# Reordering the first four feed-forward units and their transposes in a one-core attention and feed-forward kernel

## The chip, the cores and the metric

The kernel runs on one core of one Trainium2 chip. The metric is the device time of one execution in microseconds (us); the medians below are over several executions. The traces give a "span", from the first to the last instruction of the program; it is about 2 us shorter than the device time of the same execution.

Engine names: PE is TensorE, ACT ScalarE, DVE VectorE, POOL GpSimd, SP SyncE (here it only issues DMAs).

## The reference

```python
def reference(A_x, A_k_cache, A_v_cache, A_wq, A_wo, B_x, B_w_gate, B_w_up, B_w_down):
    # x: (1, 2048, 448); 16 query heads, 8 key/value heads of 256; F = 1792; all bf16
    xn = layernorm(x)
    s  = attention(xn, last 512 keys of k_cache and v_cache, wq, wo)   # [...] softmax, no mask
    g  = silu((gelu(xn @ w_gate) * (xn @ w_up)) @ w_down)
    return x + s * g
```

## The kernel before

Tokens come in 16 tiles of 128, and in 4 chunks of 512. A feed-forward *unit* is one block of 128 of the 1792 features for one chunk: 14 blocks times 4 chunks are 56 units. A unit holds two PSUM banks, one for the gate and one for the up product. Each product contracts 448 rows: three blocks of 128 (`NK = 3`) and a rest of 64. All matmuls take 64 rows, and the upper and lower half of the array work side by side on the two products. So a unit is two *passes*: the first with 8 matmuls (the rest and three blocks, two halves each), the second with 6, with the halves exchanged. For this, the rest of 64 columns of `xn` has to stand in both halves of the transposed tile `xnT`. The kernel before gets that by normalising those 64 columns twice, into a tile 512 wide:

```python
        def ln_norm(t):
            s = t % NXN
            for lo, hi, src in ((0, D, 0), (D, DP, K3)):       # 448 columns, then 64 again
                K.op("dve", lambda e, ...: e.tensor_scalar(xn[:, s, lo:hi], ...))

        def ln_tp_pe(t, b, eng):                               # tiles 0..3: transposed by PE
            for k in range(NK + 1):
                ins = e.transpose(tp[:, k * P:(k + 1) * P], xn[:, s, k * P:(k + 1) * P], ident[:, :])
            # [...] one copy PSUM -> xnT, on ACT
```

Tiles 4 to 15 are transposed by DMA (`ln_tp_dma`). At the start nothing is there yet, so three units begin at once and work through the first chunk tile by tile, in quarters of 128 columns (condensed):

```python
        warm(20, 3)                    # 20 matmuls on zeros
        ln_first(0); ln_first(1); ln_second(0); ln_second(1)
        ln_tp_pe(0, 6, "act")
        ln_stats(2); ln_std_act(2)     # a square root on ACT ahead of tile 1's copy
        ln_tp_pe(1, 7, "act")
        ln_first(3)
        HEAD, PH = (0, 1, 2), (0, 2, 4)          # units, and the first of their two banks
        gu_group(HEAD, PH, 0)                    # quarter 0 (token tile 0)
        gu_group(HEAD, PH, 1)                    # quarter 1
        # [...] DVE work
        ln_tp_pe(2, 6, "act"); ln_tp_pe(3, 7, "act")
        act(..., ACT.Gelu_apprx_tanh, ...)       # loads the Gelu table
        gu_group(HEAD, PH, 2); gu_group(HEAD, PH, 3)
        # [...]
        cur, nxt = (6, 0), (2, 4)
        for n in range(3, NU - 1, 2):            # pairs (3,4), (5,6), ...: unit 4 reuses unit 0's banks
            gu_group((n, n + 1), cur)
            gu_evac(n, cur[0])                   # Gelu on ACT, product on DVE
            ln_b()                               # normalise and DMA-transpose a coming tile
            gu_evac(n + 1, cur[1])
            ln_a()
            if n == 3:
                load_x("sp", 12, 4)
```

Unit 55 is left over and is woven into the first query heads. At the very end the last token tile's output projection runs as two halves of 224 columns, so that finishing the first half runs under the second. The program ends with `drain`: SP waits for the last DMA of each of its 16 slots, a slot being one semaphore; DMAs take the slots in turn.

The softmax here doesn't subtract the row's maximum and nothing guards it: scores larger than these inputs give would overflow.

## Time and profile before

| | |
|---|---|
| device time, median of the first 3 executions | 562.93 us (562.39 to 563.58) |
| span of the profiled execution | 560.8 us |
| PE busy | 555.0 us, 99% of the span |
| DVE / ACT / POOL busy | 279.5 / 211.5 / 32.7 us |
| chain of work that ended last | PE 98% |

These are lines of the page of the kernel before. The first two have one digit for each fortieth of the span, a tenth of full for each step: the busy share of PE, and of the DMA engines. The third is a DMA queue with its kind, packets, MB and share of the DMA engines' time. The fourth is the chain of work that ended last.

```profile
PE   8999999999999999999999999999999999999997
DMA  9910999300033034012331320144044012421331
q8 instruction: 33, 0.54, 0.4%
PE 98%; DVE 1%; DMA 0%; ACT 0%; issue 0%; DVEq 0%
```

PE is the bound everywhere, so only time in which PE starves can be won, and the only slices under 9 are the first and the last. The DMA engines are full in the first two slices (28 us). The queue called "instruction" brings PE's own program, in 33 packets of 16 KB.

This is the timeline of PE alone, before the change. The columns are start, duration, engine, line, operation, what was written and read, shape, how many were merged, and in brackets the idle time before it and what ended it.

```profile
5.71 0.40 PE L402 MATMUL bank<-ident,xn 128*128 128x128 bf16 x4 [0.18 <-DVE rstd L382]
6.79 0.23 PE L322 MATMUL bank<-xnT,wgur 64*128 64x128 bf16 x2
...
8.16 0.23 PE L322 MATMUL bank<-xnT,wgur 64*128 64x128 bf16 x2
...
9.44 0.62 PE L402 MATMUL bank<-ident,xn 128*128 128x128 bf16 x8
10.61 0.23 PE L322 MATMUL bank<-xnT,wgur 64*128 64x128 bf16 x2 [0.56 <-ACT xnT L316]
...
12.96 0.40 PE L322 MATMUL bank<-xnT,wgur 64*128 64x512 bf16 x2
13.17 0.83 PE L322 MATMUL bank<-xnT,wgu 64*128 64x512 bf16 x6
14.29 0.39 PE L322 MATMUL bank<-xnT,wgur 64*128 64x512 bf16 x2 [0.29 <-DVE actT L459]
14.52 0.81 PE L322 MATMUL bank<-xnT,wgu 64*128 64x512 bf16 x5
15.50 1.67 PE L322 MATMUL bank<-xnT,wgu 64*128 64x512 bf16 x13 [0.18 <-issue]
16.81 0.57 PE L322 MATMUL bank<-xnT,wgur 64*128 64x512 bf16 x2
...
19.84 0.57 PE L322 MATMUL bank<-xnT,wgur 64*128 64x512 bf16 x2
...
35.23 0.93 PE L322 MATMUL bank<-wd,actT 128*128 128x448 bf16 x4
```

Each group of units starts with the two matmuls on `wgur`, the rest of 64 rows, so these lines are markers: 6.79 is quarter 0, 8.16 quarter 1, 10.61 quarter 2, 12.96 the pair of units 3 and 4, 16.81 the pair 5 and 6, and from there a pair takes 3.02 us. The last line is the first work on the down weights. After the first transposes, three waits stand in the brackets: for the copies of the transposes (10.61), for the product that frees unit 0's bank (14.29), and one, at 15.50, in the middle of a unit, after the fifth of six matmuls, for nothing that the profile shows ("issue").

The end of the timeline of the kernel before, DVE's last two operations:

```profile
557.87 0.39 DVE L631 SCALAR_TENSOR_TENSOR tmp<-bank,g_58 128x224 f32<-128x224 f32 x1 [2.25 <-PE bank L322]
558.30 0.39 DVE L634 TENSOR_TENSOR ofin<-tmp,xr 128x224 bf16<-128x224 f32 x1
```

### The profile page before, as it was taken

To read this page: it belongs to the slowest core of one execution; us is meant where nothing else is said; L and a number is where in the kernel's file an instruction comes from. 1 tells how busy PE (TensorE), PEld (TensorE's weight loads), DVE (VectorE), ACT (ScalarE), POOL (GpSimd) and SP (SyncE) were. 2 spreads that over 40 slices of the span, in tenths; PEclk is the share of its full clock that TensorE was granted. 3 is DMA by queue.
4 is the path that set the end of the run, shared out by engine and by line. 5 is a ranking of instruction groups with operands and counts; after the bars stand their busy time and mean duration, and the time that the engine had idled before them with its cause. 6 is when DMAs were issued, how large, how long until landed. Compare 5 with 4: busy or idle time off the path is not lost.

```text
span 560.8 us, 9965 instructions
## 1 busy us (share of the span) xinstructions
PE 555.0 (99%) x4146; PEld 312.0 (56%) x4146; DVE 279.5 (50%) x754; ACT 211.5 (38%) x278; POOL 32.7 (6%) x64
## 2 busy tenths in 40 slices
PE   8999999999999999999999999999999999999997
PEld 6454444444566465456646745566465456656756
DVE  6775424442267466224655651267466224655622
ACT  5333323443353553304526531153553304526500
POOL 2121820000000000010000000100000010000000
PEclk9999999999999999999999999999999999999999
DMA  9910999300033034012331320144044012421331
GB/s 277 247 39 20 259 269 282 52 1 1 0 57 77 20 66 85 1 34 51 77 57 30 76 48 16 47 60 86 11 68 79 7 33 53 77 58 29 76 48 42
DMA packets 97085, 40.87 MB, mean 73 GB/s; under 512 B 85968, under 2 KB 94160, under 8 KB 97040
## 3 DMA queue, kind: packets, MB, share of 16 engines
q1 hardware_dynamic: 92976, 28.38, 25.5%
q0 software_dynamic: 3296, 11.27, 6.9%
q8 instruction: 33, 0.54, 0.4%
q10 hardware_dynamic: 768, 0.57, 0.3%
q14 instruction: 12, 0.10, 0.1%
HBM read 17.92 MB, written 1.84 MB: 35 GB/s over the span
## 4 chain that ended last, share of the span: by engine, by line
PE 98%; DVE 1%; DMA 0%; ACT 0%; issue 0%; DVEq 0%
PE bank L322 98%; DMA x_67<-in_A_x_dram 0%; DVE xn L387 0%; DVE stats L368 0%; PE bank L402 0%; DVE actT L459 0%; DVE g_58 L470 0%; ACT gl L316 0%; ACT xnT L316 0%; ACT tmp L316 0%; DVE tmp L631 0%; DVE ofin L634 0%; DVE mv L369 0%; DVE rstd L382 0%; DVEq L151 0%
## 5 line engine op out<-in xcount | busy, mean ns | idle before, releaser
L316 ACT ACTIVATE expT<-bank 128x1024 bf16<-128x1024 f32 x128 | 123.7, 1022 | 150.6 <-PE bank L322 150.5
L608 DVE TENSOR_SCALAR onorm<-bank,rden 128x256 bf16<-128x256 f32 x256 | 123.8, 484 | 9.1
L322 PE MATMUL bank<-va,expT 128*128 128x257 bf16 x1024 | 124.0, 273 | 0.0
L322 PE MATMUL bank<-qT,kT 128*128 128x512 bf16 x512 | 120.4, 379 | 0.1
L322 PEld LDWEIGHTS bank<-va,expT 128*128 128x128 bf16 x1024 | 99.2, 98 | 27.3 <-DVE onorm L608 1.3
L322 PE MATMUL bank<-wo,oT 128*128 128x448 bf16 (+1 forms) x544 | 97.6, 341 | 0.0
L322 PE MATMUL bank<-xnT,wq 64*128 64x512 bf16 x768 | 93.3, 376 | 0.0
L322 PE MATMUL bank<-xnT,wgu 64*128 64x512 bf16 (+1 forms) x780 | 83.5, 346 | 0.2 <-issue 0.2
L322 PEld LDWEIGHTS bank<-qT,kT 128*128 128x128 bf16 x512 | 49.1, 97 | 52.2 <-issue 3.4
L322 PEld LDWEIGHTS bank<-wo,oT 128*128 128x128 bf16 x544 | 53.1, 98 | 44.0
L606 DVE RECIPROCAL rden<-bank 128x1 f32<-128x1 f32 x256 | 40.9, 160 | 67.2 <-PE bank L322 67.2
L316 ACT ACTIVATE qT<-bank 128x512 bf16<-128x512 f32 x64 | 38.2, 597 | 80.7 <-PE bank L322 79.1
L581 DVE CAST qT<-bank 128x512 bf16<-128x512 f32 x64 | 42.9, 692 | 47.3 <-PE bank L322 47.3
L322 PEld LDWEIGHTS bank<-xnT,wq 64*128 64x128 bf16 x768 | 37.4, 94 | 44.7
L322 PEld LDWEIGHTS bank<-xnT,wgu 64*128 64x128 bf16 x780 | 37.7, 94 | 36.5 <-issue 0.7
L459 DVE TENSOR_TENSOR actT<-bank,gl 128x512 bf16<-128x512 f32 x56 | 37.9, 690 | 34.6 <-ACT gl L316 20.4
L316 ACT ACTIVATE gl<-bank 128x512 bf16<-128x512 f32 x56 | 33.2, 597 | 48.6 <-PE bank L322 45.4
L631 DVE SCALAR_TENSOR_TENSOR tmp<-bank,g_58 128x448 f32<-128x448 f32 (+1 forms) x17 | 10.1, 597 | 82.5 <-PE bank L322 82.5
L322 PE MATMUL bank<-wd,actT 128*128 128x448 bf16 x224 | 42.9, 353 | 0.0
L310 POOL DMA_DIRECT2D xr<-in_A_x_dram x16 | 8.6, 539 | 465.8 <-DVE ofin L634 465.8
L322 PEld LDWEIGHTS bank<-wd,actT 128*128 128x128 bf16 x224 | 21.8, 98 | 21.0 <-DVE mv L369 0.4
L470 DVE SCALAR_TENSOR_TENSOR g_58<-tmp,bank 128x448 bf16<-128x448 f32 x16 | 9.9, 622 | 33.4 <-ACT tmp L316 33.4
(35 smaller groups left out, 147.6 us busy)
## 6 DMA issues: line engine op xcount, KB each, us to landing
wo<-in_A_wo_dram POOLq DMA_DIRECT2D x4, 896.0 KB, 19.6
wq<-in_A_wq_dram POOLq DMA_DIRECT2D x2, 1536.0 KB, 10.5
va<-in_A_v_cache_dram POOLq DMA_DIRECT2D x8, 256.0 KB, 14.0
oT<-onorm SPq DMA_TRANSPOSE x128, 2.5
xr<-in_A_x_dram POOLq DMA_DIRECT2D x16, 112.0 KB, 2.3
out_dram<-ofin SPq DMA_DIRECT2D x15, 112.0 KB, 1.7
wd<-in_B_w_down_dram SPq DMA_DIRECT2D x1, 1568.0 KB, 9.4
x_67<-in_A_x_dram SPq DMA_DIRECT2D x3, 448.0 KB, 5.4
```

The costliest lines, as they stand in the source:

```text
L310: K.op(q, lambda e, o=o, i=i: e.dma_start(o, i), reads, writes, dma=True)
L316: K.op("act", lambda e, o=o, i=i: e.activation(o, i, func, scale=scale), reads, writes)
L322: ins = e.matmul(o, lhsT=l, rhs=r, start=st, stop=sp)
L459: K.op("dve", lambda e: e.tensor_tensor(actT[:, c % 2, f, :], bank[b + 1], gl[:, s, :], ALU.mult), (b_ps[b + 1], b_gl[s]), (b_actT[c % 2][ ...
L470: K.op("dve", lambda e, t=t, b=b, s=s: e.scalar_tensor_tensor(out=g2[:, t, :], in0=tmp[:, s, :], scalar=1.0, in1=bank[b][:, 0:D], op0=ALU. ...
L581: K.op("dve", lambda v, s=s, b=b: v.tensor_copy(qT[:, s, 1, :], bank[b + 1]), (b_ps[b + 1],), (b_qT[s][1],))
L606: K.op("dve", lambda e, bb=bb, r=r: e.reciprocal(rden[:, r:r + 1], bank[bb][:, Dh:Dh + 1]), (b_ps[bb],), (b_rden[r],))
L608: K.op("dve", lambda e, bb=bb, r=r, t4=t4: e.tensor_scalar(onorm[:, o, t4, h % 2, :], bank[bb][:, 0:Dh], rden[:, r:r + 1], None, op0=ALU.m ...
L631: K.op("dve", lambda e: e.scalar_tensor_tensor(out=tmp[:, s, c0:c1], in0=bank[b][:, c0:c1], scalar=0.5, in1=g2[:, t, c0:c1], op0=ALU.mult, ...
```

## The change

Its intent is to close those waits. (1) Tiles 0 to 3 are normalised once; the rest of 64 columns is transposed twice by PE, into the two halves of the output. (2) Tile 1's copy goes ahead of tile 2's square root on ACT. (3) Transposes 2 and 3 go between and after the passes of quarter 1, so that the copy of tile 2 runs under the second pass. (4) Only units 0 and 1 run quarters 2 and 3. Unit 2 does its second half in one go of 256 columns, side by side with a whole unit 3. Then all further units form pairs (4,5) to (54,55), and none is left over. (5) Gate and up weights are loaded in four blocks for three, tiles 6 and 7 of `x` after the second and third. (6) The last tile is split 320 + 128. The head on DVE and SP is reordered with it, so that tile 7's DMA transpose is issued one pair of units later.

The core of the diff:

```diff
-        for lo, hi, src in ((0, D, 0), (D, DP, K3)):
+        for lo, hi, src in ((0, D, 0), (D, DP, K3))[:1 + twice]:      # once for tiles 0..3
...
-                for k in range(NK + 1):
+                for k in range(NK):
                     ins = e.transpose(tp[:, k * P:(k + 1) * P], xn[:, s, k * P:(k + 1) * P], ident[:, :])
+                for u in range(2):
+                    ins = e.transpose(tp[R * u:R * u + R, K3:K3 + P], xn[:, s, K3:D], ident[:, :])
...
-        FBL = [0, 3, 8, NF]
+        FBL = [0, 3, 6, 9, NF]
...
         ln_tp_pe(0, 6, "act")
-        ln_stats(2)
-        ln_std_act(2)
         ln_tp_pe(1, 7, "act")
+        ln_first(2)
...
-        gu_group(HEAD, PH, 0)
-        gu_group(HEAD, PH, 1)
+        gu_group(HEAD, PH, (0, 1))
+        gu_group(HEAD, PH, (1, 2), (0,))
         ln_tp_pe(2, 6, "act")
+        gu_group(HEAD, PH, (1, 2), (1,))
         ln_tp_pe(3, 7, "act")
...
-        gu_group(HEAD, PH, 2)
-        gu_group(HEAD, PH, 3)
+        gu_group(HEAD[:2], PH[:2], (2, 3))
+        gu_group(HEAD[:2], PH[:2], (3, 4))
+        for ph in range(2):
+            gu_group(HEAD[2:], PH[2:], (2, 4), (ph,))
+            gu_group((3,), (6,), None, (ph,))
...
-        for n in range(3, NU - 1, 2):
+        for n in range(4, NU, 2):
...
-            if n == 3:
+            if n == 4:
                 load_x("sp", 12, 4)
...
-            wo_mm(3, b, 0, NCO, i * D // 2, (i + 1) * D // 2)
+            lo, hi = ((0, CUT), (CUT, D))[i]                          # CUT = 320
+            wo_mm(3, b, 0, NCO, lo, hi)
```

## The prediction

> **What bounds it.** TensorE (PE): busy 555.0 of 560.8 us, 98% of the chain that ended last, clock 1.0. Only starved stretches of PE can be won. The timeline and the waits show them, nearly all before 17 us:
>
> - Transposes of tiles 0 and 1 start at 5.71 and 6.42 us, each after two normalising DVE operations (391 + 304 ns).
> - Quarter 0 of the three head units runs from 6.79, quarter 1 from 8.15; about 0.15 us is lost between them, because ACT does tile 2's square root before it copies tile 1's transpose.
> - Transposes 2 and 3 sit after quarter 1; PE then waits for their ACT copies from 9.84 (last matmul issued) to 10.61, about 0.7 us lost.
> - Unit 4 takes unit 0's bank and waits for table load, Gelu and DVE product: 13.62 to 14.29, about 0.45 us lost.
> - A matmul in mid-unit stands still from 14.95 to 15.50, about 0.35 us, with no semaphore. The Trainium skill ("Runtime: NRT & Kernel Launch", Instruction fetch mechanics) says instructions stream in 16 KiB blocks of 256. The trace agrees in size: 33 packets of 16 KB, the first at 12.88 us. I take it for a late block.
>
> From 16.81 us pairs of units take a steady 3.02 us. The change leaves later gaps.
>
> **What the change does, costed.**
>
> 1. No second normalisation for tiles 0 to 3: tile 0 is ready 0.3 us sooner. One more transpose a tile: 0.056 us (spacing in the trace). Quarter 0 starts near 6.5: gain about 0.25 us. Weights allow that: the last piece lands at 6.22.
> 2. Tile 1's copy no longer waits behind the square root: 0.15 us.
> 3. Transposes 2 and 3 go between the passes of quarter 1, so their copies (0.59 us) run under matmuls: 0.7 us. Tiles 2 and 3 of x land at 6.42 and 6.68, so the second transpose input is ready near 9.0, in time.
> 4. Unit 2 runs its second half at 256 columns: about 0.1 us. Unit 3 runs with it in the banks left free, so the first reused bank is needed only near 14 us, after its Gelu and product (done about 13.3): 0.45 us.
> 5. Fewer instructions before the block boundary, so that stall shrinks or goes: 0 to 0.35 us, though PE also arrives there sooner. Extra transposes cost 0.1.
> 6. The last unit in a pair: nothing was starved there.
> 7. Tail 320 + 128 columns: PE 0 to 0.25 us more (128-column matmuls at 57 to 64 ns), DVE 0.2 us less (392 to about 290 ns, twice): nothing.
>
> Sum: units 0 to 3 done near 13.9 us, and the work that before was reached at 16.81 is reached near 15.4: 1.4 us, all on the critical path.
>
> **Prediction: 561.5 us, range 560.6 to 562.6.** Faster by over 2%: 0.005; within 2%: 0.99; slower by over 2%: 0.005.
>
> **What would show each step.** Timeline: quarter 0 near 6.5; no PE gap over 0.2 us at 9.5 to 10.6; no wait on the DVE product near 14; pairs at 3.02 us from about 13.9; a stall inside a unit near 15 or none. Last vector operations 0.29 us each.
>
> **What would make it wrong.** The instruction block arriving at a fixed 15.5 us, so PE merely waits there longer. Tile 7's DMA transpose, now issued one pair later (near 24.7 us), landing after unit 14 wants it (29.0): such transposes took 2.4 to 3.95 us, so margin is 0.3 us or more; a miss costs up to 1 us. Weights for unit 3 landing after 12 us. Repeats spread by 1.2 us.

## The result, and the profile after

The changed kernel took 561.93 us (median of 6, 561.63 to 564.35), the kernel before 563.25 us (median of 6, 562.39 to 564.13). Ratios here are the mean time of one kernel's runs over that of the other's of the same rounds, so not quite the ratio of the medians. This one was 0.9982, with a 95% interval of 0.9962 to 1.0002. In a second series of the unaltered kernel (below) it was 561.88 us (5 runs) against 563.26 (9 runs), ratio 0.9978, 0.9964 to 0.9991.

The one profiled execution of the first series was also the slowest, 564.35 us with a span of 562.3. The other five lay between 561.63 and 562.15. So its trace must not be read as the typical one. Its transfers were slow as a whole: between 7 and 20 us the DMA engines moved 245 GB/s, for 287 in a typical execution (after_again, below). Why is open. In that trace, PE's waits show a new line; columns are who waited for whom, us in total, times, longest:

```profile
PE bank L323 <- DMA xnT<-xn: 1.6, 1, 1.6
```

and its chain of waits near 30 us reads as follows (start, duration, what):

```profile
25.08 0.30 DVE xn L390
25.37 0.03 DVE actT L464
25.40 6.25 DMA xnT<-xn
31.65 0.09 issue
31.74 4.44 PE bank L323 x34
```

Tile 7's DMA transpose was issued at 25.40 and landed at 31.65; unit 14 needed it from about 29.9 us. This is the second danger that the prediction named, and in this execution it cost more than the change gained.

The second series has a trace of a typical execution (561.78 us, span 560.0). PE's timeline there, to be laid beside the one of before:

```profile
5.51 0.45 PE L405 MATMUL bank<-ident,xn 128*128 128x128 bf16 x3
5.89 0.25 PE L407 MATMUL bank<-ident,xn 128*64 128x128 bf16 x2
...
6.83 0.23 PE L323 MATMUL bank<-xnT,wgur 64*128 64x128 bf16 x2 [0.24 <-ACT xnT L317]
...
8.02 0.22 PE L323 MATMUL bank<-xnT,wgur 64*128 64x128 bf16 x2
...
8.78 0.34 PE L405 MATMUL bank<-ident,xn 128*128 128x128 bf16 x3
9.05 0.25 PE L407 MATMUL bank<-ident,xn 128*64 128x128 bf16 x2
9.23 0.68 PE L323 MATMUL bank<-xnT,wgu 64*128 64x128 bf16 x18
9.84 0.34 PE L405 MATMUL bank<-ident,xn 128*128 128x128 bf16 x3
10.12 0.25 PE L407 MATMUL bank<-ident,xn 128*64 128x128 bf16 x2
10.29 0.23 PE L323 MATMUL bank<-xnT,wgur 64*128 64x128 bf16 x2
...
14.30 0.38 PE L323 MATMUL bank<-xnT,wgur 64*128 64x512 bf16 x2
14.52 0.81 PE L323 MATMUL bank<-xnT,wgu 64*128 64x512 bf16 x6
15.16 0.38 PE L323 MATMUL bank<-xnT,wgur 64*128 64x512 bf16 x2
...
32.53 3.77 PE L323 MATMUL bank<-wd,actT 128*128 128x448 bf16 x19
```

After 6.83 no bracket is left: neither the copies (10.29), nor a bank (14.30), nor the standstill inside a unit. Units 4 and 5 start at 14.30, and unit 5 follows at 15.16 without a break. The first work on the down weights, a fixed point later, came at 35.23 us after 17 units before, and at 32.53 us after 16 units here. One unit is half a pair, 1.51 us, so the gain up to there is 35.23 - 32.53 - 1.51 = 1.19 us. PE's last matmul starts 1.18 us sooner as well (556.40 for 557.58): the stages between give nothing back. (The list of PE's waits has eight short ones for ACT `qT` here, 1.3 us in all; 36 matmul records are missing from this trace, and the complete traces of tp_after_q1 and warm60 have no such waits.) Yet the span is only 0.8 us shorter (559.99 for 560.79). The end lost 0.38 us. DVE's last two operations of the same execution:

```profile
556.66 0.29 DVE L639 SCALAR_TENSOR_TENSOR tmp<-bank,g 128x128 f32<-128x128 f32 x1 [0.77 <-PE bank L323]
556.98 0.29 DVE L642 TENSOR_TENSOR ofin<-tmp,xr 128x128 bf16<-128x128 f32 x1
```

They are 0.1 us shorter each, as intended. From the landing of the last store to the end of the program, however, it took 1.22 us for 0.53.

### The profile page after: what moved, and what is told of

It is laid out like the page before. It is cut to its first block, busy times and chain, and to the rows that moved or that the text cites. A ratio compares the mean times of both kernels' runs of the same rounds, so it can differ in the third digit from the quotient of the medians. Undisturbed runs are those within 1.5% of the kernel's fastest.

```text
span 562.3 us, 9907 instructions
## 1 busy us (share of the span) xinstructions
PE 552.8 (98%) x4100; PEld 310.7 (55%) x4136; DVE 278.5 (50%) x750; ACT 211.7 (38%) x278; POOL 32.8 (6%) x64
## 4 chain that ended last, share of the span: by engine, by line
PE 96%; DMA 2%; DVE 1%; ACT 1%; issue 1%; DVEq 0%
PE bank L323 95%; DMA xnT<-xn 1%; DMA x_67<-in_A_x_dram 0%; ACT qT L317 0%; DVE stats L371 0%; PE bank L405 0%; DVE xn L390 0%; DVE g_58 L475 0%; ACT gl L317 0%; ACT xnT L317 0%; DVE actT L464 0%; ACT tmp L317 0%; PE bank L407 0%; DVE mv L372 0%; DVE tmp L639 0%
## 5 line engine op out<-in xcount | busy, mean ns | idle before, releaser
L323 PE MATMUL bank<-qT,kT 128*128 128x512 bf16 x476 | 115.8, 379 | 2.8 <-ACT qT L317 1.3
L323 PE MATMUL bank<-wo,oT 128*128 128x448 bf16 (+2 forms) x544 | 97.6, 341 | 0.0
L639 DVE SCALAR_TENSOR_TENSOR tmp<-bank,g_58 128x448 f32<-128x448 f32 (+2 forms) x17 | 10.1, 597 | 82.3 <-PE bank L323 82.3
```

The costliest lines, as they stand in the source:

```text
L323: ins = e.matmul(o, lhsT=l, rhs=r, start=st, stop=sp)
L639: K.op("dve", lambda e: e.scalar_tensor_tensor(out=tmp[:, s, c0:c1], in0=bank[b][:, c0:c1], scalar=0.5, in1=g2[:, t, c0:c1], op0=ALU.mult, ...
```

## The experiments

There were twelve runs, all correct; two of them repeat a kernel without an edit. Each was timed in five rounds against the kernel before; "span" is that of its profiled execution.

| run | median us | ratio to before (95%) | span |
|---|---|---|---|
| after_again | 561.88 | 0.9978 (0.9964 to 0.9991) | 560.0 |
| x12_late | 561.88 | 0.9977 (0.9965 to 0.9990) | 559.9 |
| warm10 | 561.66 | 0.9974 (0.9962 to 0.9987) | 559.9 |
| warm30 | 562.56 | 0.9988 (0.9975 to 1.0000) | 561.0 |
| tp_after_q1 | 562.18 | 0.9979 (0.9963 to 0.9994) | 560.1 |
| join_undone | 562.36 | 0.9982 (0.9964 to 0.9999) | 560.5 |
| warm60 | 562.88 | 0.9992 (0.9976 to 1.0008) | 561.1 |
| drain_sorted | 561.78 | 0.9977 (0.9958 to 0.9996) | 559.5 |
| warm30_x12 | 561.90 | 0.9977 (0.9964 to 0.9989) | 560.2 |
| tail_half | 562.06 | 0.9979 (0.9965 to 0.9992) | 560.1 |
| best | 561.30 | 0.9968 (0.9955 to 0.9980) | 559.5 |
| before_again | 562.98 | 0.9995 (0.9982 to 1.0007) | 560.8 |

They ran in three series on different chips, of four runs each in the order of the table; the kernel before had medians of 563.26, 563.16 and 563.23 us in them, so medians of different series can be compared to about 0.1 us. The first four runs are in the series of after_again. The intervals of single ratios are as wide as most effects here.

### 1. The changed kernel again (after_again)

No edit.

> The changed kernel once more, unaltered. In its first profile tensor tile 7's DMA transpose landed at 31.65 us and PE stood still for 2.0 us before unit 14, and that one execution was 2.2 us longer (564.35) than the other five (561.63 to 562.15). Theory A (the transpose is late in every execution that is profiled or not): the gap before unit 14 shows again, 1 to 2 us, and the new profiled run is about as long as the unprofiled ones. Theory B (a chance event, or an effect of profiling): the gap is gone or the profiled run is again about 2 us longer than the rest. The stall after the 219th matmul (449th instruction of PE) should show again at 0.3 to 0.6 us under the block theory. Time 561.6 to 562.3.

Measured: 561.88 us; the profiled execution took 561.78, no longer than the rest. Tile 7's transpose was issued at 24.86 us, landed at 28.46, and unit 14 began at 29.41: 0.95 us to spare and no gap. There was no standstill at the 219th matmul either, which the expectation had wrong. So theory B holds, in its first form: the late transpose of the first trace was the chance of one long execution, not an effect of profiling. Single executions about 2 us longer than their series also turned up once for the kernel before (566.06) and once in drain_sorted (563.98), without a trace, so their causes are open.

### 2. Less traffic ahead of tile 7's transpose (x12_late)

```diff
-            if n == 4:
+            if n == 8:
                 load_x("sp", 12, 4)
```

> The changed kernel, with the load of x tiles 12 to 15 issued after tile 7's transpose (unit pair 8,9) and not ahead of tile 6's (pair 4,5). Theory: transposes of tiles 6 and 7 wait in the traffic of the down weights and of this load on the same queue; 0.46 MB less ahead of them is worth about 1.7 us, so tile 7 lands near 30 us instead of 31.65 and the gap before unit 14 shrinks from 2.0 us to 0.3 or less in the profile. Rival: it is the down weights alone (1.6 MB) that delay it: gap stays over 1.2 us. Time of unprofiled runs: the same as the changed kernel if these runs have no such gap, otherwise 0.5 to 1.5 us less.

Measured: 561.88 us, no change. Tile 7 landed at 27.29 us, 1.2 us sooner than in after_again, with about 2.0 us to spare before unit 14 at 29.29. The typical execution had no gap to close, so this buys only margin. The expectation spoke of the long execution, which did not come back.

### 3. and 4. Moving the instruction block (warm10, warm30)

```diff
-                ins = e.matmul(bank[b][:, 0:256], lhsT=gl[:, 0, 0:P], rhs=gl[:, 0, 0:256], ...)
+                ins = e.matmul(bank[b][:, 0:512], lhsT=gl[:, 0, 0:P], rhs=gl[:, 0, 0:512], ...)   # warm10
+                ins = e.matmul(bank[b][:, 0:170], lhsT=gl[:, 0, 0:P], rhs=gl[:, 0, 0:170], ...)   # warm30
-        warm(20, 3)
+        warm(10, 3)                                                                               # warm10
+        warm(30, 3)                                                                               # warm30
```

> The changed kernel, with 10 warming matmuls of 512 columns for 20 of 256: the same columns in 20 fewer instructions. Block theory (PE stands still when its 512th instruction with about 63 before the kernel's own, that is the kernel's 449th, has not been fetched): the boundary moves 10 matmuls later in the work, into the pair of units 6 and 7, which PE reaches 2.5 us later than the block can arrive; no stall near 15 us, units 6,7 begin near 17.2 rather than 17.68, about 0.45 us gained. Rival (a stall tied to a time or to the DMA load near 15.5 us): it stays at 0.3 to 0.6 us in units 4,5.

> The changed kernel, with 30 warming matmuls of 170 columns: the same columns in 20 more instructions. Block theory: the boundary (449th instruction) falls 10 matmuls earlier in the work, in the second pass of unit 3, which PE reaches near 13.2 us; the block arrives near 15.3 to 15.8, so a stall of about 2 us right after the 219th matmul, and units 6,7 begin near 19: about 1.5 us lost against the changed kernel. Rival (tied to a time): stall of the old size near 15.3 us, in another place of the work, and no time lost.

Measured, warm10: 561.66 us, no standstill. But the changed kernel has none in a typical execution either, so this tells nothing apart.

Measured, warm30: 562.56 us, 0.7 more, but not for the reason expected. At the 219th matmul the rhythm broke by only 0.1 us. PE's timeline shows it as a `wgur` pair that takes 0.48 us and not 0.38:

```profile
14.27 0.48 PE L323 MATMUL bank<-xnT,wgur 64*128 64x512 bf16 x2
```

My figure of 2 us was wrong because I put the 219th matmul too early in the work: it is the first of unit 4, at 14.27 us. The block was also there sooner than the 15.3 to 15.8 us that I had assumed. The 0.7 us (1.0 in the profiled execution, 562.75) came from another place: a gap before unit 14, of 1.1 us, until tile 7's transpose landed at 30.29 us (issued at 24.92). The profile does not name the transpose there:

```profile
30.38 0.39 PE L323 MATMUL bank<-xnT,wgur 64*128 64x512 bf16 x2 [0.73 <-issue]
```

### 5. Many more instructions (warm60)

The same edit with `warm(60, 3)` and 85 columns: the same columns to stream, 80 more instructions.

> The changed kernel with 60 warming matmuls of 85 columns: the same columns in 80 more instructions. With 30 of them the spacing at the 219th matmul was broken by 0.1 us at exactly that place (14.27 us). Block theory: the boundary now falls at the 219th or 220th matmul, at the start of unit 2's long half, which PE reaches near 11.9 us, while the block is there 1.45 us after its 16 KB packet ends, near 12.8 to 14.2: a stall of 0.8 to 2.3 us right there, and the kernel longer by as much (562.7 to 564). Rival (the broken spacing has another cause): no gap over 0.3 us at the 219th or 220th matmul and the time within 0.3 us of the changed kernel.

Measured: 562.88 us, and the standstill, in PE's timeline:

```profile
11.33 0.74 PE L323 MATMUL bank<-xnT,wgu 64*128 64x128 bf16 x18
13.13 0.28 PE L323 MATMUL bank<-xnT,wgur 64*128 64x256 bf16 x2 [1.06 <-issue]
```

It came after the 220th matmul, at the start of unit 2's long half, 1.2 us, exactly where the block theory had it. Counting PE's instructions settles which place that is. A matmul is two instructions, a weight load and a multiplication, and waits count as well. In the traces of the kernel before, of the changed kernel's first execution and of warm30, PE has started 219 multiplications, 220 weight loads and 10 others when it stands still, which is 449 instructions; in warm60 they are 220, 221 and 8, which is 449 again. The place in the work and the time differ, the instruction number does not. With the packet times of the instruction queue from the traces (first packet after the start, us):

| trace | packet | PE goes on | after the packet's end | standstill |
|---|---|---|---|---|
| before | 12.88 to 13.95 | 15.50 | 1.56 | 0.55 |
| before_again | 12.91 to 14.01 | 15.56 | 1.55 | 0.64 |
| after, first (long) trace | 13.26 to 14.42 | 15.93 | 1.51 | 0.67 |
| warm30 | 11.73 to 12.98 | 14.38 | 1.40 | 0.10 |
| warm30_x12 (below) | 11.93 to 13.20 | 14.52 | 1.31 | 0.10 |
| warm60 | 10.60 to 11.78 | 13.13 | 1.35 | 1.22 |
| after_again | 11.40 to 12.70 | 15.38, not held up | 2.68 | none |

The standstill is the spacing of two matmul starts less the spacing that they usually have (0.003 us within a pair of array halves, 0.05 between pairs of short ones). PE goes on 1.31 to 1.56 us after the packet is through; where PE comes later than that, there is none. That it is the late block is shown by this, by warm60 above all. The 0.10 of warm30 is weaker: warm30_x12 has the same 0.10 with a packet that ended 0.23 us later, so it need not measure how late the block was. Why the first packet starts near 11.3 us in typical executions of the changed kernel and at 12.9 in both traces of the kernel before is not isolated. It was 11.20 in join_undone, which has the new loads and the old order of units, so the order of units is not the cause. The new order and size of the weight loads, which share the full DMA engines, is the likely one, but that is only argued, and it is not the whole of it: the long execution of the changed kernel had the new loads and its first packet at 13.26.

### 6. Tile 7 and the 30 warming matmuls (warm30_x12)

The edits of warm30 and of x12_late together.

> The changed kernel with 30 warming matmuls of 170 columns and the load of x tiles 12 to 15 issued after tile 7's transpose. With the 30 alone, tile 7's transpose landed at 30.29 us, PE stood still for 1.1 us before unit 14, and the time was 562.56 against 561.88. Theory: that 0.7 us is the late transpose and nothing else; with less traffic ahead the transpose lands before 28 us, the gap before unit 14 is gone and the time is back at 561.8 to 562.1. Rival: the 20 extra instructions cost it by later instruction blocks: the gap stays, or the time stays above 562.3.

Measured: 561.90 us, and no gap before unit 14. Tile 7 landed at 29.34 us, later than I had expected (28) but in time. The block cannot have been the cause of warm30's gap, since the next boundary is 256 instructions on, some 13 matmuls before unit 14, and the rhythm is unbroken there. So 0.7 us of warm30 was the late transpose. Why that transpose was slower in warm30 (5.4 us from issue to landing, for 3.6 in after_again) stays open; more PE instructions alone do not do it, since it took 3.2 us in warm60.

### 7. The transposes back behind quarter 1 (tp_after_q1)

```diff
-        gu_group(HEAD, PH, (1, 2), (0,))
+        gu_group(HEAD, PH, (1, 2))
         ln_tp_pe(2, 6, "act")
-        gu_group(HEAD, PH, (1, 2), (1,))
         ln_tp_pe(3, 7, "act")
```

> The changed kernel with the transposes of tiles 2 and 3 put back after both passes of quarter 1. Theory: PE waits again for the ACT copy of tile 2, a gap of 0.7 us near 10 us, and the start of units 4,5 moves from about 14.2 us to about 14.8; all later work follows, so 0.5 to 0.7 us longer than the changed kernel (562.4 to 562.6). Rival: something later (the instruction block, tile 7's transpose) absorbs it, and the time changes by less than 0.2 us.

Measured: 562.18 us, 0.3 over after_again. PE's timeline:

```profile
9.16 0.34 PE L405 MATMUL bank<-ident,xn 128*128 128x128 bf16 x3
9.44 0.25 PE L407 MATMUL bank<-ident,xn 128*64 128x128 bf16 x2
9.62 0.34 PE L405 MATMUL bank<-ident,xn 128*128 128x128 bf16 x3
9.89 0.25 PE L407 MATMUL bank<-ident,xn 128*64 128x128 bf16 x2
10.47 0.23 PE L323 MATMUL bank<-xnT,wgur 64*128 64x128 bf16 x2 [0.33 <-ACT xnT L317]
```

Quarter 2 starts at 10.47, for 10.17 in x12_late, whose head is that of the changed kernel and whose quarter 0 starts in the same place (6.71). So the new place is worth 0.30 us and not 0.5 to 0.7. The wait is only 0.33 us here and not 0.7, since the copy of tile 2 already runs while tile 3 is transposed. A set of transposes is long now, in either place. Here tile 3's first transpose starts 0.45 us after tile 2's (9.16 to 9.62); between the passes, in after_again, the next matmuls start 0.45 us after tile 2's first transpose (8.78 to 9.23). Two sets so cost 0.9 us of PE time, where the eight full transposes of the kernel before cost 0.45 (9.44 to the last start at 9.84, and one spacing of 0.056). What makes a set dear is the two transposes of 64 columns: the first of them starts 0.149 us after the full one ahead of it, and the next work 0.176 us after the second, for 0.056 between full ones.

### 8. The old order of units (join_undone)

The hunks of point (4) of the change, and the loop over pairs from unit 3 with unit 55 woven into the query heads, set back; all else as changed.

```diff
-        gu_group(HEAD[:2], PH[:2], (2, 3))
-        gu_group(HEAD[:2], PH[:2], (3, 4))
-        for ph in range(2): ...                    # unit 2's half with unit 3
+        gu_group(HEAD, PH, (2, 3))
+        gu_group(HEAD, PH, (3, 4))
-        for n in range(4, NU, 2):
+        for n in range(3, NU - 1, 2):
```

> The changed kernel, with the third unit in four quarters like the first two, pairs starting at unit 3 (units 3,4 in banks 6,7,0,1) and the last unit interleaved with the first query heads, as before the change. Theory: unit 4 waits for table load, Gelu and product of unit 0 on bank 0: a gap of 0.4 to 0.5 us near 13.5 us on PE, and no gap at the end of the units; total 0.4 to 0.6 us longer than the changed kernel (562.3 to 562.5). Rival: the gain of the change lies in the transposes alone, and this costs under 0.2 us.

Measured: 562.36 us, 0.5 more. PE's timeline has the wait for the product again:

```profile
13.02 0.81 PE L323 MATMUL bank<-xnT,wgu 64*128 64x512 bf16 x6
14.12 0.39 PE L323 MATMUL bank<-xnT,wgur 64*128 64x512 bf16 x2 [0.29 <-DVE actT L464]
```

Matmul starts are 0.667 us apart there, usual is 0.213: 0.45 us, as the prediction had it. The run as a whole does not measure this wait alone. PE's last matmul is 0.60 us later than in x12_late; 0.24 of that is the late clock at the start (quarter 0 at 6.95 for 6.71), and the rest, 0.36 us, is near the 0.31 us of the wait less what the shorter form of unit 2 saves (0.15, see the ledger).

### 9. The split of the last tile (tail_half)

```diff
-    CUT = D - P
+    CUT = D // 2
```

> The changed kernel with the last token tile split at 224 columns again. Theory: PE's time for the tile is the same (6.13 us either way in the traces), the last two DVE operations take 0.39 us each for 0.29, so the span grows by 0.2 us and the median by 0.1 to 0.3. Rival: the wider rows of the last store (448 bytes for 256) or the end of program gain it back, no change.

Measured: 562.06 us, span 560.15 for 559.85 in x12_late with PE's last matmuls at the same place. DVE's last two operations took 0.39 us each again, and the wider last store 0.07 us more from issue to landing. So the split is worth the 0.2 us that DVE gains, and a little of the store; PE's two column groups took 6.30 us from first start to last end (6.13 up to where a next matmul could start) either way.

### 10. The order of the waits at the end (drain_sorted)

```diff
-        for (e, s), o in self.last_dma.items():
+        for (e, s), o in sorted(self.last_dma.items(), key=lambda kv: kv[1].idx):
```

> The changed kernel with the end of program on SP reordered: it waits for its 16 DMA slots in the order of their last issue, not of the slots' numbers. In the changed kernel the last store's slot was waited for second of eight that the trace shows at the end, with six further waits of 0.07 us after it landed; before the change there was one. Theory: the end comes 0.35 to 0.45 us sooner after the last store lands (1.2 us to about 0.8) and the time falls by about 0.4 us, to about 561.5. Rival: those waits overlap with something else that ends the program, no change.

Measured: 561.78 us with one long execution of 563.98; without it the mean is 561.73, against 561.91 in after_again. These are the last of SP's records, start and end in us, from the traces (waits that were over before are left out, but for those of drain_sorted):

```
after_again   557.75 558.79  wait (the last store lands at 558.77)
              558.83 558.86  wait, and five more up to 559.17
              559.23 559.27  branch
              559.71 559.78  drain               program ends 559.99
drain_sorted  557.67 557.70  wait, and five more up to 558.01
              558.70 558.72  wait (the last store lands at 558.68)
              558.79 558.83  branch
              559.25 559.33  drain               program ends 559.54
before        559.48 560.28  wait (the last store lands at 560.26)
              560.32 560.34  wait
              560.38 560.42  branch
              560.56 560.57  drain               program ends 560.79
```

From landing to end: 0.53 us before, 1.22 after the change, 0.87 with sorted waits. The change does not touch these waits, but it issues five more DMAs on SP, so the last store fell into another slot, and six waits for slots that were long free came behind it, about 0.065 us each. The sorted order takes 0.36 us off in the trace; the times show some 0.1 to 0.2 of it. The rest, the pause between branch and drain of 0.42 to 0.43 us for 0.14, stays. A packet of 8 KB of instructions appears near the end of most of the changed kernel's traces, but only after the pause is over (at 560.30 us in after_again), and also in before_again, where the pause is 0.13 us. So it does not explain the pause, whose cause is open.

### 11. All repairs together (best)

warm10, x12_late and drain_sorted in one kernel.

> The changed kernel with all three repairs: 10 warming matmuls of 512 columns, the load of x tiles 12 to 15 after tile 7's transpose, and the end waits on SP in the order of last issue. Theory: 0.1 to 0.4 us less than the changed kernel in typical executions (561.5 to 561.8), all of it from the end waits, and no stall at the instruction block or before unit 14 even in a slow execution. It would be the fastest of all, by an amount near the noise. Rival: the typical time is the changed kernel's, 561.9.

Measured: 561.30 us (561.27 to 561.93), the fastest of all, ratio to before 0.9968. It never ran in the same rounds as the changed kernel; against the same kernel before, that one had 0.9978 and 0.9982. Its trace has the first down product at 32.41 us, as x12_late has, no standstill, and 0.86 us from the last landing to the end. So what is shown of its gain is the 0.36 us at the end.

### 12. The kernel before again (before_again)

No edit.

> The kernel before, once more with a profile. Its first profile had a stall of 0.34 us at the 219th matmul. The changed kernel had one of 0.46 us in its first profile and none in its second. Theory: the block comes late only in some executions, whether it lands before PE needs it being a matter of a few tenths: with the 16 KB packet ending before about 13.5 us there is no stall here either. If the stall is there again with a packet that ended before 13.5 us, the theory of 1.45 us between packet and resumption is wrong. Gaps near 10 us (0.77 us between matmul starts) and near 14 us (0.67) should show again within 0.1 us.

Measured: 562.98 us. The standstill in mid-unit is there again:

```profile
14.48 0.81 PE L322 MATMUL bank<-xnT,wgu 64*128 64x512 bf16 x5
15.55 1.67 PE L322 MATMUL bank<-xnT,wgu 64*128 64x512 bf16 x13 [0.26 <-issue]
```

The packet ended at 14.01 us, and PE went on 1.55 us later, in the first trace 1.56. So the late block belongs to the kernel before in both of its traces, and its absence belongs to the change in typical executions. "Only in some executions" was wrong for this kernel. The gaps near 10 and 14 us came back to the hundredth (0.774 and 0.668 us between starts).

## Why the prediction was right

The total was right: 561.5 us was predicted, with 560.6 to 562.6, and 561.93 and 561.88 were measured. The forecast gain of 1.4 us compares with 1.3 and 1.4 us between the medians, about 1.0 and 1.2 us by the ratios, and 0.8 us between the spans of two typical traces. Several of its terms were wrong and cancelled, so that the total came out so close is partly luck; the range allowed for it. The terms as listed even add up to 1.55 to 1.9 us, while the prediction put down 1.4. The ledger compares the kernel before with x12_late, which has the head of the changed kernel and starts quarter 0 where the traces mostly do, at 6.71 (after_again: 6.83, where the full clock came 0.8 us later).

| step of the prediction | predicted, us | measured, us | from |
|---|---|---|---|
| 1, quarter 0 sooner | 0.25 | 0.08 | 6.79 to 6.71 |
| 2, tile 1's copy ahead of the square root | 0.15 | 0.18 | quarter 0 lasts 1.19 for 1.37 |
| 3 with the extra transposes of 5 | 0.7 - 0.1 | 0.18 | quarter 2 starts at 10.17 for 10.61, less the two above; tp_after_q1: 0.30 for the place alone |
| 4, longer form of unit 2 | 0.1 | -0.15 | quarters 2 and 3 and the rest of unit 2: 2.50 for 2.35 |
| 4, wait for unit 0's bank | 0.45 | 0.46 | gap at 14 us gone; join_undone: 0.45 |
| 5, late instruction block | 0 to 0.35 | 0.55 | table above |
| up to PE's last matmul | about 1.4 | 1.31 | 557.58 to 556.27 |
| 7, the tail | 0 | -0.4 | landing to end 1.22 for 0.53; DVE and store 0.3 less |

- *Step 1* was mis-sized. DVE was 0.2 us sooner (transposes from 5.50 for 5.71), but I counted one more transpose at the usual spacing of 0.056 us. With the two transposes of 64 columns, the time from the first transpose to the start of the copy rose from 0.43 to 0.56 us.
- *Step 3*, with the extra transposes, was the largest error, and it lay in the cost of the transposes. The wait did go: 0.72 us. But the two sets cost 0.90 us of PE for 0.45 before, where the prediction put 0.1 for the extra ones, and quarter 1, broken up by them, lasts 1.37 us for 1.28. 0.72 less 0.45 less 0.09 is the 0.18 of the table. No run kept the second normalisation and moved the transposes alone, which would have kept the shorter sets.
- *Step 4*: the bank was right. The saving on short matmuls had the wrong sign: a quarter of two units takes 0.87 us where one of three took 1.17 to 1.18, so a matmul costs 31 ns for 28, and the 256-column matmuls do not make up for it.
- *Step 5*: mechanism right, size wrong. The matmul that stands still is the second of a pair and is due 0.003 us after the first, not 0.2, so the standstill is 0.55 us. The broken rhythm lasts to the end of the stage: 0.83 us of the two waits shows at once (the pair 3, 4 took 3.85 us for 3.02), the last 0.19 only when the stage ends. The chance of an absent standstill was underrated, since I took the packet to start at a like time; in typical executions it started 1.5 us sooner, for which the prediction gave no reason.
- *Step 7*: PE even and DVE 0.2 us faster, as said. The waits at the end were not on the list at all.
- *Step 6* was not separated from step 4; the traces show no starved time at the end of the units in either kernel.
- *The dangers.* Tile 7's transpose was issued at 24.86 (predicted 24.7) and landed 0.95 us early in a typical execution, 1.8 us late in one: a loss larger than the "up to 1 us" of the prediction, in the only execution that was profiled at first. The trace of the kernel before held the warning: there the transposes of tiles 6 and 7 took 7.0 and 6.6 us from issue to landing (tile 7: 21.62 to 28.25), and the 2.4 to 3.95 us of the prediction leave them out. The instruction block at a fixed time did not come true in typical executions; in that long one it was later still (15.93). Unit 3's weights landed at 9.79 us in after_again, in time.

The prediction leaned on the Trainium skill ("Runtime: NRT & Kernel Launch", Instruction fetch mechanics) for the blocks of 16 KiB and 256 instructions. The runs agree: packets of 16,384 bytes, and a standstill after 449 instructions of the kernel wherever the packet was late. That is 512 = 2 times 256 if 63 instructions run ahead of the kernel's own, which no run shows directly.

## What to carry to other kernels

When a change removes a wait, count what the work around it costs afterwards as well: here a wait of 0.72 us went, but transposes that had been changed for another reason took 0.45 us more of PE, and 0.18 us was left. Also check on the trace how much of the wait would be overlapped in any case: moving the transposes alone gave 0.30 us. A standstill of PE in the middle of a run of matmuls, for nothing that the profile names, can be its own program arriving late while the DMA engines are full; count instructions and see whether it stays at one number when the work moves. After any change in the number of DMAs look at the end of the program too, and wait last for the DMA that was issued last.

## What the Trainium skill lacked or had wrong

- "Runtime: NRT & Kernel Launch", Instruction fetch mechanics, calls the cost of a block boundary "mostly hidden". While the DMA engines were full it was not: 0.55 and 0.64 us in the two traces of the kernel before, 1.2 us in warm60, and PE went on 1.31 to 1.56 us after the packet's end.
- The same section gives PE 128 KiB of instruction memory (2048 instructions), and further down says that it is two lines of 16 KiB. The standstill after 449 instructions of the kernel, in five kernels, fits two blocks of 256 loaded ahead, if 63 instructions run ahead of the kernel's own; it does not fit eight.
- "TensorE: Matmul & The Clock Gate", Part 4: PE-mode transpose, gives about 275 ns as the duration of a transpose in a kernel's context. In the trace of the kernel before it is 221 ns (mean of 16), and full transposes in a row start 0.056 us apart. What mattered was the set: three full ones and two of 64 columns took 0.45 us of PE time. Part 4 has no figure for the spacing or for such a set.
- No page that I found has what the kernel's own waits at the end of a program cost: about 0.065 us for each semaphore wait on SP that follows the last landing, and an unexplained 0.14 or 0.43 us between the branch and the drain.
- "DMA: Bandwidth & Descriptors" gives a bandwidth for DMA transposes, 261 GB/s, but not how much the time of a small one varies under load: the same 128-token transpose of tile 7 took 2.5 to 6.6 us from issue to landing in these traces.
